# Linear attention feeding a SiLU layer: 64-position blocks with paired heads, a planned order, and casting transfers

## The chip, the cores and the metric

The kernel runs on one core of a Trainium2 chip. The metric is the device time of one execution in microseconds, the median of several runs; lower is better. The names of the engines are those of the profile: PE multiplies matrices (PEld loads its weights), DVE, ACT and POOL work on elements, SP only issues transfers. ACT and POOL can issue transfers too. Each engine takes its instructions in the order in which the program lists them.

## The reference

Two computations follow each other. The first is attention with a decay per head, worked off in blocks of positions with a state carried from block to block; the second is a two-layer network on its output. Inputs and output are float32; batch 4, 8 heads, 768 positions, 64 features per head, then 3072 rows of 512 features with 2048 in between.

```python
for b in range(nb):                                   # block = 64 positions
    intra = einsum('bhic,bhjc->bhij', qb, kb) * Dmask # lam ** (i - j) where i >= j, else 0
    intra = einsum('bhij,bhjd->bhid', intra, vb)
    inter = einsum('bhid,bhde->bhie', qb * lam_pow, kv_state)   # lam ** (i + 1)
    out[:, :, sl] = intra + inter
    kv_state = lam ** 64 * kv_state + einsum('bhsd,bhse->bhde', kb * rev_pow, vb)  # lam ** (63 - s)
x = out.transpose(0, 2, 1, 3).reshape(3072, 512)
h = x @ w_in
result = (h * sigmoid(h)) @ w_out
```

## The kernel before

**Units.** The work is cut into 24 units u of 128 positions with all 8 heads: four batches of six. The kernel takes 128 positions as one attention block, which is the same function as two blocks of 64. Two heads share the 128 partitions, so there are four pairs (NP = 4).

**Per unit.** `load` (L60) issues three transfers of 256 KB on SP (q, k, v in float32, runs of 64 features, 256 bytes each). `prep` multiplies q and k by powers of lam into bf16 on DVE (L157, L159) and copies v into a zero-padded tile on ACT (L161). `T` transposes q and k on PE, 8 times 128 columns (L169), and ACT copies the result out (L174, and L178 into the zero-padded `kTz`). `ST` computes scores per head, 8 matmuls of 128 columns (L193), and DVE applies the mask (L199). `OUT` multiplies scores by v, 8 matmuls (L217), adds the carried state, 4 matmuls except in a batch's first unit (L221), and ACT copies the sum into `xt` (L229), the activations of the network, transposed. `STATE` computes the new state in 4 matmuls (L245); DVE adds the old one (L254, L256) and POOL scales it (L260, L263); a batch's last unit has no state to pass on.

**The network.** Positions are taken in chunks of 512, four units. `gemm1` makes one 128-feature slice of the hidden layer: four matmuls of 512 columns (L278), then Silu on ACT (L284). `gemm2` makes 128 rows of output: 16 matmuls of 512 columns (L297), a copy on DVE (L303) and a store on SP (L305).

**Weights.** They are loaded as float32 on SP in eight pieces of 1 MB (L70, L75) into four staging buffers and cast to bf16 by DVE (L144, L147). A staging buffer comes free when its cast is done.

**Order.** It is written by hand: four units of attention first, then the first product for chunk 0 mixed with units 4 to 7, then for each chunk n the first product of n, the second of n - 1 and the attention of the units of n + 1, item by item. PSUM's 8 banks are dealt out for good: transposes 1, scores 2, outputs 1, state 1, first product 2, second 1.

```python
cast_w_in(0)
run(g1(0, range(0, 2)))
...
for n in range(1, NCH):
    for t in range(UPC):
        u = (n + 1) * UPC + t
        if u < NU:
            run(both(n, t), unit(u))
```

Of the kernel before, what the change touches and what calls it, by code (L numbers as in the profile page):

```python
# [7 lines left out]
F32 = mybir.dt.float32  # L8
BF16 = mybir.dt.bfloat16
AF = mybir.ActivationFunctionType  # L10
AL = mybir.AluOpType


@with_exitstack
def kernel(
# [13 lines left out]
    BLK = 128  # L29
    NB = S // BLK  # L30
    NU = B * NB
    NP = H // 2
    DM = moe_w_in.shape[0]
    DFF = moe_w_in.shape[1]
    assert DM == H * D == 512 and DFF == 2048
    KI = DM // 128
    KO = DFF // 128
    CH = 512
    NCH = B * S // CH
    UPC = CH // BLK  # L40

    ctx.enter_context(tc.manual_schedule())
    const = ctx.enter_context(tc.tile_pool(name="const", bufs=1))
    raw = ctx.enter_context(tc.tile_pool(name="raw", bufs=8))
    stage = ctx.enter_context(tc.tile_pool(name="stage", bufs=4))
    work = ctx.enter_context(tc.tile_pool(name="work", bufs=3))
    gpool = ctx.enter_context(tc.tile_pool(name="gpool", bufs=36))
    opool = ctx.enter_context(tc.tile_pool(name="opool", bufs=3))
    ps = ctx.enter_context(tc.tile_pool(name="ps", bufs=1, space=bass.MemoryType.PSUM))


    raws = {}

    def load(u):
        b, blk = divmod(u, NB)
        sl = slice(blk * BLK, (blk + 1) * BLK)
        tiles = []
        for name, src in (("qf", q), ("kf", k), ("vf", v)):
            t = raw.tile([128, H, 64], F32, tag=name, name=name)
            nc.sync.dma_start(out=t, in_=src[b, :, sl, :].rearrange("h s d -> s h d"))  # L60
            tiles.append(t)
        raws[u] = tiles

    w_in_r = moe_w_in.rearrange("(ko p) f -> p ko f", p=128)
    w_out_r = moe_w_out.rearrange("(ko p) f -> p ko f", p=128)
    wstage = {}

    def load_w_in(j):
        t = stage.tile([128, KI, 512], F32, tag="wst", name="w_st")
        nc.sync.dma_start(out=t, in_=w_in_r[:, :, j * 512:(j + 1) * 512])  # L70
        wstage["i", j] = t

    def load_w_out(j):
        t = stage.tile([128, 4, DM], F32, tag="wst", name="w_st")
        nc.sync.dma_start(out=t, in_=w_out_r[:, 4 * j:4 * j + 4, :])  # L75
        wstage["o", j] = t

    lam_sb = const.tile([128, H], F32)
    nc.sync.dma_start(
# [3 lines left out]
    for u in range(4):  # L83
        load(u)
    load_w_in(0)
    load_w_in(1)
    load(4)
    load_w_in(2)
    load(5)
    load_w_in(3)  # L90
    load(6)
    load(7)


    iota_i = const.tile([128, 1], mybir.dt.int32)
    nc.gpsimd.iota(iota_i, pattern=[[0, 1]], base=-64, channel_multiplier=1)
    pos = const.tile([128, 1], F32)
    neg = const.tile([128, 1], F32)
    nc.vector.tensor_copy(pos, iota_i)
    nc.vector.tensor_scalar(neg, pos, -1.0, None, op0=AL.mult)  # L100
    ident = const.tile([128, 128], BF16)
# [5 lines left out]
    mask = const.tile([128, BLK], F32)  # L107
    nc.gpsimd.memset(mask, 1.0)
    nc.gpsimd.affine_select(
        out=mask, in_=mask, compare_op=AL.is_ge, fill=0.0,  # L110
        base=0, pattern=[[1, BLK]], channel_multiplier=-1,
    )

    NKT, NVP, NX = 3, 4, 2
    kTz = [const.tile([128, NP, 2, BLK], BF16, name=f"kTz{i}") for i in range(NKT)]
    vz = [const.tile([128, NP, 4, 64], BF16, name=f"vz{i}") for i in range(NVP)]
    Xz = [const.tile([128, NP, 128], BF16, name=f"Xz{i}") for i in range(NX)]
    for i in range(max(NKT, NVP, NX)):
        if i < NKT:
            nc.vector.memset(kTz[i], 0.0)  # L120
        if i < NVP:
            nc.gpsimd.memset(vz[i], 0.0)
        if i < NX:
            nc.gpsimd.memset(Xz[i], 0.0)

    log_lam = const.tile([128, H], F32)
    nc.scalar.activation(log_lam, lam_sb, AF.Ln)
    lam_fwd = const.tile([128, H], F32)
    lam_bwd = const.tile([128, H], F32)
    nc.scalar.activation(lam_fwd, log_lam, AF.Exp, scale=pos[:, 0:1])  # L130
    nc.scalar.activation(lam_bwd, log_lam, AF.Exp, scale=neg[:, 0:1])
    lam_blk = const.tile([128, NP, 64], F32)
    for hh in range(2):
        r = slice(64 * hh, 64 * hh + 64)
        nc.scalar.activation(
            lam_blk[r, :, :], log_lam[r, hh::2][:, :, None].to_broadcast([64, NP, 64]),
            AF.Exp, scale=float(BLK),
        )

    w_in_bf = const.tile([128, KI, DFF], BF16)  # L140
    w_out_bf = const.tile([128, KO, DM], BF16)

    def cast_w_in(j):
        nc.vector.tensor_copy(w_in_bf[:, :, j * 512:(j + 1) * 512], wstage["i", j])  # L144

    def cast_w_out(j):
        nc.vector.tensor_copy(w_out_bf[:, 4 * j:4 * j + 4, :], wstage["o", j])  # L147


    qs, ks, qT, sts, Xf = {}, {}, {}, {}, {}  # L150
    xts = {}

    def prep(u):
        qf, kf, vf = raws.pop(u)
        qs[u] = work.tile([128, H, 64], BF16, tag="qs", name="qs")
        ks[u] = work.tile([128, H, 64], BF16, tag="ks", bufs=4, name="ks")
        nc.vector.tensor_tensor(  # L157
            qs[u], qf, lam_fwd[:, :, None].to_broadcast([128, H, 64]), op=AL.mult)
        nc.vector.tensor_tensor(  # L159
            ks[u], kf, lam_bwd[:, :, None].to_broadcast([128, H, 64]), op=AL.mult)  # L160
        nc.scalar.activation(  # L161
            vz[u % NVP][:, :, 0:4:3, :], vf.rearrange("p (a b) d -> p a b d", b=2), AF.Copy)

    def T(u):
        out_l = []
        tr = ps.tile([128, 2 * NP, BLK], BF16, tag="tr", name="tr")
        for i in range(2 * NP):
            src = (qs if i < NP else ks)[u].rearrange("p (a b) d -> p a (b d)", b=2)
            out_l.append((1, lambda i=i, src=src: nc.tensor.transpose(  # L169
                tr[:, i, :], src[:, i % NP, :], ident)))  # L170

        def evac():
            qT[u] = work.tile([128, NP, BLK], BF16, tag="qT", name="qT")
            nc.scalar.activation(qT[u], tr[:, 0:NP, :], AF.Copy)  # L174
            kz = kTz[u % NKT]
            for hh in range(2):
                r = slice(64 * hh, 64 * hh + 64)
                nc.scalar.activation(kz[r, :, hh, :], tr[r, NP:2 * NP, :], AF.Copy)  # L178
        out_l.append((0, evac))
        return out_l  # L180

    def ST(u):
        out_l = []
        kz = kTz[u % NKT]
        for half in range(2):
            box = {}

            def first(box=box):
                box["ps"] = ps.tile([128, 4, BLK], F32, tag="st", bufs=2, name="st_ps")
            out_l.append((0, first))  # L190
            for i in range(4):
                h = 4 * half + i
                out_l.append((1, lambda i=i, h=h, box=box: nc.tensor.matmul(  # L193
                    box["ps"][:, i, :], lhsT=kz[:, h // 2, h % 2, :], rhs=qT[u][:, h // 2, :],
# [246 lines left out]
```

## Time and profile before

| what | value |
|---|---|
| median of 3 runs | 256.36 us (255.65 to 257.78) |
| span of the profiled execution, first to last instruction | 254.5 us |
| HBM read, written | 27.27 MB, 6.29 MB |
| DMA packets | 82,722, of which 75,536 under 512 bytes |
| PE, 512-column matmuls (L278, L297) | 384 and 384 |
| PE, 128-column matmuls | 736 |
| ACT, Silu (L284) | 96 x 596 ns |

The profile is of one execution. Its span runs from the first to the last instruction of the program; of the execution as timed only the runs above are given. Busy times are the union of an engine's instructions; a matmul's listed length (379 ns for 512 columns) contains its way through the array, in which the next one already runs, so the listed lengths of PE add up to more than its time. A row of groups names the line, the engine, the operation, output and inputs, the count and shape, then busy time, mean length in ns, and idle time before it with what ended it.

### The profile page before, as it was taken

Reading aid. Unit: us, or ns where it says so; the run is one execution under the profiler, and the core shown is the slowest. Engines: PE = TensorE matmul, PEld = TensorE weight load, DVE = VectorE, ACT = ScalarE, POOL = GpSimd, SP = SyncE. Lnnn points to the kernel's source line nnn. Section 1 sums busy time; section 2 is a strip of 40 time slices with the busy share of each in tenths; the row PEclk is TensorE's granted clock in tenths of the full one; section 3 lists DMA queues with packets and bytes.
Section 4 is the critical chain, followed back from the end, with each engine's and each line's share of the span. In section 5 each row is a group of like instructions: output and inputs, shape, how many; then the busy total and the mean of one; then the engine's idle time right before and its main releaser. Section 6 shows DMA issues by size and latency. Waiting matters only on the chain.

```text
span 254.5 us, 3814 instructions
## 1 busy us (share of the span) xinstructions
PE 219.0 (86%) x1504; PEld 120.7 (47%) x1504; DVE 117.9 (46%) x173; ACT 126.9 (50%) x224; POOL 56.7 (22%) x71
## 2 busy tenths in 40 slices
PE   0664875937785999999999999999999999999994
PEld 0553343515442555555555555555555544444441
DVE  3586648357808537362574382537632410111221
ACT  6566374646643465656555755665465333333000
POOL 8056402004404411040343120404421200000000
PEclk9999597988999999999999999999999999999999
DMA  6999999999999994466347110111011101111122
GB/s 131 219 260 321 279 267 230 342 197 284 222 265 212 237 254 117 94 169 152 79 101 165 44 41 1 45 41 44 0 41 44 39 2 41 44 41 41 41 85 82
DMA packets 82722, 33.81 MB, mean 133 GB/s; under 512 B 75536, under 2 KB 75536, under 8 KB 82704
## 3 DMA queue, kind: packets, MB, share of 16 engines
q1 hardware_dynamic: 82704, 33.57, 55.0%
q8 instruction: 12, 0.20, 0.3%
q14 instruction: 6, 0.05, 0.1%
HBM read 27.27 MB, written 6.29 MB: 132 GB/s over the span
## 4 chain that ended last, share of the span: by engine, by line
PE 66%; DVE 1%; ACT 0%; issue 0%
PE o_ps L297 26%; PE h_ps L278 25%; PE st_ps L297 5%; PE x_ps L217 3%; PE st_ps L193 2%; PE tr L169 2%; PE x_ps L221 1%; PE d_ps L245 1%; DVE o_sb L303 1%; DVE st_sb L199 1%; ACT g L284 0%; ACT xt L229 0%
## 5 line engine op out<-in xcount | busy, mean ns | idle before, releaser
L278 PE MATMUL h_ps<-xt,w_in_bf 128*128 128x512 bf16 x384 | 119.0, 392 | 9.9 <-ACT g L284 7.2
L284 ACT ACTIVATE g<-h_ps 128x512 bf16<-128x512 f32 x96 | 57.2, 596 | 80.7 <-PE h_ps L278 80.3
L297 PE MATMUL o_ps<-w_out_bf,g 128*128 128x512 bf16 x320 | 91.4, 379 | 2.1 <-DVE w_out_bf L147 1.9
L260 POOL TENSOR_TENSOR Xz<-y,lam_blk 64x256 bf16<-64x256 f32 x40 | 34.4, 861 | 141.9 <-DVE y L256 88.3
L278 PEld LDWEIGHTS <-w_in_bf 128*128 128x128 bf16 x384 | 38.2, 100 | 44.0 <-issue 6.9
L297 PEld LDWEIGHTS <-g 128*128 128x128 bf16 x384 | 37.4, 98 | 43.9
L217 PE MATMUL x_ps<-st_sb,vz 128*128 128x128 bf16 x192 | 37.1, 227 | 8.6 <-DVE st_sb L199 7.5
L193 PE MATMUL st_ps<-qT,kTz 128*128 128x128 bf16 x192 | 36.4, 231 | 4.5 <-ACT kTz L178 4.2
L199 DVE TENSOR_TENSOR st_sb<-st_ps,mask 128x512 bf16<-128x512 f32 x48 | 31.3, 686 | 9.3 <-PE st_ps L193 8.8
L256 DVE TENSOR_TENSOR y<-d_ps,Xf 64x256 f32<-64x256 f32 x32 | 13.5, 422 | 41.0 <-PE d_ps L245 35.1
L303 DVE COPY o_sb<-o_ps 128x512 f32<-128x512 f32 x20 | 13.8, 691 | 31.8 <-PE o_ps L297 31.7
L178 ACT ACTIVATE kTz<-tr 64x512 bf16<-64x512 bf16 x48 | 28.1, 586 | 0.6
L157 DVE TENSOR_TENSOR qs<-qf,lam_fwd 128x512 bf16<-128x512 f32 x24 | 19.6, 817 | 15.1 <-DMA qf<-in_q_dram 12.2
L217 PEld LDWEIGHTS <-vz 128*128 128x128 bf16 x192 | 18.5, 102 | 14.1 <-issue 7.5
L159 DVE TENSOR_TENSOR ks<-kf,lam_bwd 128x512 bf16<-128x512 f32 x24 | 24.1, 1003 | 2.4 <-DMA kf<-in_k_dram 2.3
L193 PEld LDWEIGHTS <-kTz 128*128 128x128 bf16 x192 | 18.3, 103 | 12.6 <-ACT kTz L178 6.5
L169 PE MATMUL tr<-ident,qs 128*128 128x128 bf16 x96 | 17.8, 232 | 6.2 <-DVE qs L157 6.2
L161 ACT ACTIVATE vz<-vf 128x512 bf16<-128x512 f32 x24 | 15.1, 629 | 12.2 <-DMA vf<-in_v_dram 12.2
L174 ACT ACTIVATE qT<-tr 128x512 bf16<-128x512 bf16 x24 | 14.3, 595 | 9.5 <-PE tr L169 9.4
L169 PE MATMUL tr<-ident,ks 128*128 128x128 bf16 x96 | 17.4, 227 | 0.2 <-DVE ks L159 0.2
L221 PE MATMUL x_ps<-qT,Xz 128*128 128x128 bf16 x80 | 17.0, 219 | 0.3
L263 POOL TENSOR_TENSOR Xf<-y,lam_blk 128x256 f32<-128x256 f32 x16 | 16.6, 1036 | 1.3
(32 smaller groups left out, 108.6 us busy)
## 6 DMA issues: line engine op xcount, KB each, us to landing
qf<-in_q_dram SPq DMA_DIRECT2D x24, 256.0 KB, 5.0
kf<-in_k_dram SPq DMA_DIRECT2D x24, 256.0 KB, 5.1
vf<-in_v_dram SPq DMA_DIRECT2D x24, 256.0 KB, 5.1
out_dram<-o_sb SPq DMA_DIRECT2D x24, 256.0 KB, 2.0
w_st<-in_moe_w_in_dram SPq DMA_DIRECT2D x4, 1024.0 KB, 7.4
w_st<-in_moe_w_out_dram SPq DMA_DIRECT2D x4, 1024.0 KB, 7.9
lam_sb<-in_lam_dram SPq DMA_DIRECT2D x1, 4.0 KB, 2.8
```

What stands on the lines that cost most here:

```text
L157: nc.vector.tensor_tensor(qs[u], qf, lam_fwd[:, :, None].to_broadcast([128, H, 64]), op=AL.mult)
L159: nc.vector.tensor_tensor(ks[u], kf, lam_bwd[:, :, None].to_broadcast([128, H, 64]), op=AL.mult)
L169: out_l.append((1, lambda i=i, src=src: nc.tensor.transpose(tr[:, i, :], src[:, i % NP, :], ident)))
L178: nc.scalar.activation(kz[r, :, hh, :], tr[r, NP:2 * NP, :], AF.Copy)
L193: out_l.append((1, lambda i=i, h=h, box=box: nc.tensor.matmul(box["ps"][:, i, :], lhsT=kz[:, h // 2, h % 2, :], rhs=qT[u][:, h // 2, :], s ...
L199: nc.vector.tensor_tensor(t, box["ps"], mask[:, None, :].to_broadcast([128, 4, BLK]), op=AL.mult)
L217: out_l.append((1, lambda p=p, hh=hh, h=h: nc.tensor.matmul(box["ps"][:, p, :], lhsT=vp[:, p, hh, :], rhs=sts[u, h // 4][:, h % 4, :], sta ...
L221: out_l.append((1, lambda p=p: nc.tensor.matmul(box["ps"][:, p, :], lhsT=Xz[u % NX][:, p, :], rhs=qT[u][:, p, :], start=False, stop=True)))
L260: nc.gpsimd.tensor_tensor(xz[r, :, r], y[r], lam_blk[r], op=AL.mult)
L278: out_l.append((1, lambda ko=ko: nc.tensor.matmul(box["ps"], lhsT=w_in_bf[:, ko, m * 128:(m + 1) * 128], rhs=xts[n][:, ko, :], start=(ko = ...
L284: nc.scalar.activation(gs[n, m], box["ps"], AF.Silu)
L297: out_l.append((1, lambda ko=ko: nc.tensor.matmul(box["ps"], lhsT=gs[n, ko][:, t * 128:(t + 1) * 128], rhs=w_out_bf[:, ko, :], start=(ko = ...
```

## The change

**Attention in blocks of 64.** A unit stays 128 positions, but is computed as two blocks c of 64. For k and v, the 128 partitions now hold 64 positions of two heads, one head in each half; `kb` and `vb` are bf16 tiles whose off-diagonal halves are zero, so that one matmul serves a pair of heads: a weight of 128 x 128, block-diagonal, and a right-hand side of 64 columns. Scores are 8 such matmuls per unit, outputs 8, states 8 (4 in a batch's last unit), carried states 8 (4 in its first). The decay moves from q and k into the mask, into `lam_k` on v (`vd`, DVE) and into `lam_x` when the output is copied into `xt` (DVE).

**Transfers.** k and v of a unit come in 4 transfers of 64 KB each on SP, cast to bf16 on DVE or ACT into `kb` and `vb`. q and all eight pieces of the weights are transferred by POOL straight into bf16 tiles. For units 0 to 7 q and k are transposed on PE (12 times 128 columns); from unit 8 on two transposing transfers on SP do it, from SBUF to SBUF. Stores are issued by ACT.

**Groups.** The first product is done for groups of 1, 1, 1, 1, 2, 2, 2, 2, 4, 4, 4 units, with 128, 256 or 512 columns per matmul, four, two or one slices of the hidden layer to a PSUM bank. The second product of the last unit is split into two halves of 256 columns, each with its own copy.

**Order.** Every matmul, copy and transfer is a task with a key (its place in a rough order of units), the engines that may do it with a duration for each, what it depends on, and the buffers it holds. A list scheduler in the kernel's code walks through these with its own clock and, whenever an engine is free, takes the ready task with the lowest key; the tasks are then issued in that order. It also picks the engine where there is a choice. PSUM's 8 banks are one pool.

```diff
+    LAT = {"PE": 0.23, "ACT": 0.06, "DVE": 0.06, "POOL": 0.08, "SP": 0.0}
...
+    TURNED = 8
+    POOLS = dict(bank=8, qb=8, kf=6, vf=6, kb=4, qkT=4, vb=5, vd=4, st=3, xb=4, y=3, xf=3,
+                 xt1=4, xt2=2, xt4=2, g=40, osb=4)
...
-            nc.sync.dma_start(out=t, in_=src[b, :, sl, :].rearrange("h s d -> s h d"))
+            nc.sync.dma_start(out=t[halves[h], c], in_=src[b, h, s0 + 64 * c:s0 + 64 * c + 64])
+            nc.gpsimd.dma_start(out=fixed_tile(bufs[0]), in_=q[b, :, s0:s0 + U, :].rearrange("h s d -> s h d"))
...
-        t = stage.tile([128, KI, 512], F32, tag="wst", name="w_st")
-        nc.sync.dma_start(out=t, in_=w_in_r[:, :, j * 512:(j + 1) * 512])
-        nc.vector.tensor_copy(w_in_bf[:, :, j * 512:(j + 1) * 512], wstage["i", j])
+                nc.gpsimd.dma_start(out=w_in_bf[:, :, cs], in_=w_in_r[:, :, cs])
+                nc.gpsimd.dma_start(out=w_out_bf[:, 4 * j:4 * j + 4, :], in_=w_out_r[:, 4 * j:4 * j + 4, :])
+    sequence = ["u0", "u1", "i0", "u2", "i1", "u3", "i2", "i3", "u4", "u5", "o0", "u6", "o1", "u7", "o2", "o3"]
+    sequence += [f"u{u}" for u in range(8, NU)]
...
+    groups = [[0], [1], [2], [3], [4, 5], [6, 7], [8, 9], [10, 11]] + [list(range(4 * n, 4 * n + 4)) for n in range(3, NU // 4)]
...
+            if u < TURNED:
+                    nc.tensor.transpose(t[:, j - n0, :], turn_source(j), ident)
+            else:
+                    nc.sync.dma_start_transpose(t_of()[:, n0:n1, :], i.rearrange(
+                        "p h d -> p (h d)" if src is qb else "p i g d -> p (i g d)"))
...
-                    box["ps"][:, i, :], lhsT=kz[:, h // 2, h % 2, :], rhs=qT[u][:, h // 2, :],
+            nc.tensor.matmul(t[:, c, a, :], lhsT=t_of()[:, 4 + NP * c + a, :],
+                             rhs=t_of()[:, a, 64 * c:64 * c + 64], start=True, stop=True)
+            mult(e, tile_of(st, [128, 2, NP, 64], BF16, "st"), st_ps.tile,
+                 mask[:, None, :, :].to_broadcast([128, 2, NP, 64]))
+            nc.tensor.matmul(t[:, c, a, :], lhsT=fixed_tile(kb)[:, i],
+                             rhs=vd.tile[:, i, :], start=True, stop=True)
...
+                prev = add((s + ko / 16, 2), {"PE": w / 2400 + 0.0025}, lambda e, ko=ko, f=mm: f(e, ko),
+                           deps=[ta, prev] + wload["o", ko // 4], bufs=[bank, g])
+                nc.scalar.dma_start(out=out[128 * u:128 * u + 128, cs], in_=osb.tile[:, cs])
...
+    for _, _, e, t in plan.order():
+        t.fn(e)
```

The core of the scheduler, cut:

```python
for e in free:
    ...
    while ready[e]:
        key, i, t = heapq.heappop(ready[e])
        ...
        if any(len(self.pools[p]) < n for p, n in need.items()):
            kept.append((key, i, t))
            continue
        mine = now + t.on[e]
        if any(max(free[o], now) + d < mine - 1e-9 for o, d in t.on.items() if o != e):
            kept.append((key, i, t))
            continue
        took = t
        break
    ...
    free[e] = now + t.on[e]
    t.end = free[e] + self.LAT[e]
    if t.nbytes:
        dma = max(dma, free[e] + 1.3) + t.nbytes / t.rate
        t.end = dma + 0.7
```

## The prediction

> **What bounds the kernel now.** I read the first two parts of the page, then the costliest groups, the windows, and the timeline of PE and of the SP queue.
>
> ```profile
> span 254.5 us, 3814 instructions
> ...
> PE 219.0 (86%) x1504; PEld 120.7 (47%) x1504; DVE 117.9 (46%) x173; ACT 126.9 (50%) x224; POOL 56.7 (22%) x71
> ...
> PE   0664875937785999999999999999999999999994
> ...
> PEclk9999597988999999999999999999999999999999
> DMA  6999999999999994466347110111011101111122
> ```
>
> PE is ragged up to about 85 us, while DMA is full, and solid afterwards. The windows (columns: PE, PEld, DVE, ACT, POOL busy us with counts, granted clock, DMA share, GB/s):
>
> ```profile
> 0.00:26.00 26.00, 11.59 (x124) 9.06 (x124) 16.64 (x30) 16.49 (x28) 13.93 (x26) 0.97 1.11 232
> 26.00:58.00 32.00, 22.42 (x147) 12.54 (x148) 18.00 (x23) 17.27 (x32) 4.41 (x4) 0.82 1.03 265
> 58.00:90.00 32.00, 24.46 (x193) 14.30 (x192) 20.86 (x29) 15.90 (x30) 11.35 (x12) 0.99 1.14 242
> 90.00:215.00 125.00, 124.75 (x877) 68.75 (x876) 56.85 (x85) 69.51 (x123) 27.02 (x30) 1.00 0.30 75
> 215.00:250.00 35.00, 35.00 (x163) 15.84 (x162) 4.84 (x7) 7.76 (x13) 0.00 (x0) 1.00 0.14 53
> ```
>
> From 90 to 250 us PE waits for nothing. What a matmul occupies there is the distance to the next start, not its listed length: 0.216 us for 512 columns, 0.056 us for 128. The page counts 768 of the first (384 + 320 + 64) and 736 of the second: 165.9 + 41.2 = 207.1 us of PE work. The last matmul ends at 250.8 us, so 250.8 - 207.1 = **43.7 us are lost, all before 90 us** (the granted clock, 0.82 in the second row, is part of it), and 3.7 us follow the last matmul. Whatever gains must cut PE work or that early loss.
>
> **The change part by part.**
>
> *PE, products.* Same columns, other cuts. Two starts give a straight line in columns (128: 0.056, 512: 0.216), so 256 take 0.109. First product: 4 groups of one unit, 256 x 0.056 = 14.3; 4 pairs, 256 x 0.109 = 27.9; 3 fours, 192 x 0.216 = 41.5; together 83.7. Second: 23 x 16 x 0.216 = 79.5, and the last unit in halves 32 x 0.109 = 3.5; 83.0. Before: 165.9; after: 166.7.
>
> *PE, attention.* 192 transposes become 8 units x 12 = 96, 5.4 us. The other 544 matmuls of 128 columns become 736 of 64 (scores 192, outputs 192, states 4 x (5 x 8 + 4) = 176, carried 4 x (4 + 40) = 176), each still with a 128-column weight load. No 64-column matmul stands in the trace. The line gives 0.029; no gain from the narrower right-hand side would be 0.056. Between them one place speaks:
>
> ```profile
> 16.83 0.39 PE L245 MATMUL d_ps<-vz,ks 128*128 128x128 bf16 x4
> 17.01 0.10 PEld L193 LDWEIGHTS <-kTz 128*128 128x128 bf16 x1
> 17.05 0.22 PE L193 MATMUL st_ps<-qT,kTz 128*128 128x128 bf16 x1
> ```
>
> The four L245 started 0.056 apart, the last at 17.00. The next load began only at 17.01, yet its matmul went at 17.05, its regular turn. So a load needs at most 0.04 us before its matmul. I take 0.034, between 0.029 and 0.04: 736 x 0.034 = 25.0 us. Sum after: 166.7 + 5.4 + 25.0 = **197.1 us**, 10.0 less than before; with 0.029, 193.4; with 0.056, 213.3, which is more than before.
>
> The Trainium skill, "TensorE: Matmul & The Clock Gate", section "LDWEIGHTS (loading the stationary operand)", gives a load of P columns P/1.2 ns, 107 ns here. Matmuls that each bring a load start 56 ns apart in this trace, so the measurement speaks against that figure. By it the 736 would take 78.5 us and the run 276 us.
>
> *Start.* What feeds it is DMA:
>
> ```profile
> 7.00 1.14 SPq L60 DMA_DIRECT2D qf<-in_q_dram  x1
> 8.19 1.10 SPq L60 DMA_DIRECT2D kf<-in_k_dram  x1
> 9.32 1.32 SPq L60 DMA_DIRECT2D vf<-in_v_dram  x1
> 10.69 1.14 SPq L60 DMA_DIRECT2D qf<-in_q_dram  x1
> ```
>
> A unit (three loads of 256 KB) goes through in 3.6 us. For weights: up to 76 us the GB/s of the windows add up to 19.2 MB; less 8.4 MB of weights that is 13.7 units, 49.5 us, leaving some 24.5 us for 8 weights, 3.07 each. The new order u0 u1 i0 u2 i1 u3 i2 i3 u4 u5 o0 u6 o1 u7 o2 o3 then lands, from 2 us on: i0 at 12.3, u3 at 22.5, u4 at 32.3, o3 at 55.3. What PE can do per unit, by the prices above: attention 1.05 + 0.67 of transposes = 1.7; a quarter of the first product 0.9; of the second 0.86. Before u3 is there, that is three units' attention (5.1) and two quarters for three units (5.4): 10.5 us. Lost at that point: landing 22.5, plus the way from landing to `xt`, less 10.5. The way: the sum of bare rows (cast 0.42, transposes 0.4, copy out 0.7, scores 0.3, mask 0.69, outputs 0.3, `xt` 0.69, handing on) is 4 us; before, unit 0's v landed at 7.5 and its `xt` began at 15.4, 8 us. I take 7: 19 us. The other points give less (u4: 32.3 + 7 - 21.2 = 18). With some queueing I put the **loss at 20 us** in place of 43.7; its ends are 12 (landing alone) and 43.7 (nothing won). Most of the gain is that the first product starts per unit, not per four units after L144's cast, and that no weight waits for a staging buffer (the last is issued only at 67.94 us now) or for DVE: PE's waits there (L144 2.5, L147 1.9) and 10.4 us of DVE casts go.
>
> What must stay hidden: early DVE and ACT work. Per unit: casts of k and v 4 x 0.42 (a quarter of L144's 1.39 plus a start), scaled v 0.69 to 1.0, copies out of the transposes about 1.1, mask 0.69, states 0.84, spreading 4 x 0.29, `xt` 0.69, 7 us together, and Silu 4 x 0.6: 9.4 us on two engines, 4.7 each, against 6.7 us per unit (53.3 / 8) that DMA needs with the weights. It fits, but not loosely: each us that these engines need per unit beyond 6.7 would add 8 us over the 8 early units.
>
> *Queues.* SP gets 192 loads of 64 KB and 32 transposing transfers instead of 105 transfers. The shortest SP issue is 0.33 to 0.43 us, so 8 loads cost 2.9 us per unit, less than 3.6. A transposing transfer waits for its cast, and the next units' loads stand behind it; those have 8.2 us of PE work per unit (197.1 / 24) to hide in. No transposing row exists; the same bytes as a load take 1.14 + 0.57 = 1.7 us per unit, below zero is excluded since PE's share of it is already counted. I take that, hidden. ACT gets the stores: 25 x 0.4 = 10 us of an engine busy half the time; Silu stands behind each. POOL gets 32 issues; nearest rows: SP's 0.4, POOL's own longest operation 1.59 and a load's landing 5.0. I take 1.6: 16 of them, 26 us, end long before 55.3. One table load (1.28 us) goes.
>
> *End.* The last copy is halved: 0.69 to 0.42, so 3.4 us after the last matmul.
>
> *Sum.* 197.1 + 20 + 3.4 = 220.5 us of span, and 0.7 for small waits of the new order (the old one has none after 90 us): 221.2. Only the span of the profiled execution is given; the median of the timed runs, 256.36, lies 1.8 above 254.5. So **223 us**.
>
> **The rivals.**
>
> *Weight loads set the pace.* If a 64-column matmul takes 0.056 us, PE work is 213.3 and the time 239. For it: every load is still 128 columns and listed with 98 ns. Against it: the 0.04 above. 0.10. The page's 107 ns, which the trace contradicts, has 0.01 and 276.
>
> *POOL holds up the start.* If a casting transfer occupies POOL until it lands, at 5.0 us for q and 7.4 to 7.9 for weights (the page's landing times), q6 lands at 2 + 7 x 5.0 + 4 x 7.4 + 7.9 = 74.5 us, when 37 us of work have been enabled, and the loss becomes 74.5 + 7 - 37 = 44.5: 247 us. For it, POOL's Xf takes 0.73 us at 20.02 with DVE elsewhere and 1.59 at 27.12 behind a DVE cast:
>
> ```profile
> 25.07 3.06 DVE L144 CAST w_in_bf<-w_st 128x2048 bf16<-128x2048 f32 x2
> ...
> 27.12 1.59 POOL L263 TENSOR_TENSOR Xf<-y,lam_blk 128x256 f32<-128x256 f32 x1
> ```
>
> Against it: those weight casts go, and the remaining ones are 0.4 us. The Trainium skill, "SBUF — State Buffer", section "SBUF: two separate sides", says that GpSimd cannot write descriptors while VectorE runs a two-port copy; the trace agrees so far that POOL's work doubles. 0.13.
>
> *Transposing transfers bind: slower.* If each holds the SP queue until it has landed (5.1 us, the landing of 256 KB), a unit costs SP 2 x 5.1 + 2.9 = 13.1 us against 8.2 of PE. 16 units from 55 us on, then 36 (the last four units' products 28, the way to `xt` and the end 8): 55 + 210 + 36 = 301 us. It decides from (256 - 91) / 16 = 10.3 us per unit, 3.7 per transfer. For it: SP blocked 5.26 us on one load at 18.08. Against it: there it was queued behind weights on a full DMA; later DMA is at 0.30. 0.08.
>
> *The order is no better.* The written-in durations miss and PE, which takes its instructions in order, waits at heads of lists as much as before: 197.1 + 43.7 + 3.4 + 1.8 = 246 and 10 us of new waits spread over 24 units, 256. Nothing after 90 us hints at it. 0.05.
>
> **How the numbers follow.** Forecast 0.60 at 223; weight pace 0.10; POOL 0.13; transposing 0.08; no better 0.05; 107 ns 0.01; a start better than 211, 0.03. Low end: 0.029 (-3.7) and a loss of 12 (-8): 211. High end: 247, with the POOL rival in. About a sixth is left out (transposing, no better, 107 ns, a better start). Measurement of this kernel tells about 1% from no change: faster 0.60 + 0.10 + 0.13 + 0.03 = 0.86; same 0.04 (most of "no better"); slower 0.10.
>
> **What would show it.** Starts of 64-column matmuls 0.03 to 0.04 apart; first product beginning near 13 us; PE solid from about 50 us; POOL issues under 3 us; SP never the last releaser of a score matmul after 60 us; DMA full to about 55 us. The forecast is wrong if PE has holes after 60 us, or if scores wait for `qkT`.

## The result, and the profile after

The changed kernel takes **283.31 us** (median of 4 runs, 282.12 to 284.6), the kernel before 256.0 us on the same chip (4 runs): a ratio of 1.104, interval 1.097 to 1.111. The forecast was 223 us, with 0.86 for faster; the time lies above the range and on the other side.

First the page of the changed kernel: span, busy times, the 40 slices, the queues, and the two lines of the chain that ended last.

```profile
span 282.9 us, 5054 instructions
...
PE 214.6 (76%) x1936; PEld 133.9 (47%) x1936; DVE 116.7 (41%) x251; ACT 123.8 (44%) x233; POOL 44.1 (16%) x65
...
PE   0563997998089961986620199999999999999994
...
PEclk9998797999659995699595589999999999999999
DMA  7999999994465499458456597997451001010113
...
q1 hardware_dynamic: 77824, 18.89, 38.6%
q0 software_dynamic: 29184, 7.34, 26.3%
...
PE 37%; SPq 7%; DMA 3%; DVE 2%; issue 2%; ACT 1%; ACTq 0%; DVEq 0%
```

Before, PE was ragged to 85 us and solid afterwards. Now it has holes up to the 23rd slice (163 us), whole slices at 0 to 2 tenths among them, and is solid only from there. The windows (the columns as before) show where:

```profile
26.00:58.00 32.00, 26.43 (x390) 22.43 (x391) 20.12 (x42) 16.80 (x32) 8.92 (x11) 0.85 1.54 175
58.00:90.00 32.00, 22.25 (x218) 15.78 (x216) 15.05 (x33) 12.80 (x24) 2.15 (x3) 0.84 0.59 125
90.00:120.00 30.00, 21.46 (x157) 12.59 (x156) 11.43 (x27) 10.58 (x20) 5.05 (x6) 0.83 0.91 132
120.00:150.00 30.00, 17.42 (x193) 12.12 (x191) 12.98 (x29) 10.73 (x21) 1.22 (x2) 0.86 0.60 123
150.00:180.00 30.00, 17.78 (x163) 12.30 (x163) 10.33 (x22) 11.50 (x21) 4.34 (x5) 0.74 0.73 126
180.00:215.00 35.00, 34.81 (x360) 19.26 (x358) 27.95 (x57) 26.07 (x52) 8.20 (x11) 1.00 0.78 131
```

None of the five columns is near full between 58 and 180 us, and where PE is short, DVE, ACT and POOL are short too. That is the look of everybody waiting for one late thing, not of a busy engine.

The prediction's two quantities can be read again. PE's work is **193.4 us**: 64-column matmuls start 29 ns apart (median of 602 neighbouring pairs of one line), and 128, 256 and 512 columns keep 56, 109 and 216 ns. The last matmul starts at 278.65 us, so 85.2 us are lost, where before it was 43.6 (43.7 in the forecast, counted to the end of the last matmul). The loss up to a time is that time less the work of the matmuls started by then:

| us | 30 | 60 | 70 | 80 | 90 | 120 | 140 | 160 | 180 | end |
|---|---|---|---|---|---|---|---|---|---|---|
| before | 21.1 | 34.9 | 38.8 | 42.3 | 43.3 | 43.4 | 43.3 | 43.4 | 43.2 | 43.6 |
| after | 23.9 | 31.8 | 32.4 | 41.6 | 43.4 | 54.7 | 62.7 | 80.6 | 84.8 | 85.2 |

Three pieces, then: about 32 us up to 60 us, 9 us in one hole at 70 to 80, and 42 us after 90, of which before had none. In the terms of the forecast's sum: PE work 193.4 us for 197.1, loss 85.2 for 20 and 0.7 of small waits, and 4.2 from the last start to the end, together 282.9 us of span.

**The late piece.** The longest hole ends at 161.7 us. The chain of waits leading to it (start, length, what):

```profile
142.56 0.61 SPq L277
143.28 1.27 SPq L371
144.65 1.23 SPq L371
145.98 0.60 SPq L277
...
157.06 3.28 DMA qkT<-kb
160.51 0.56 issue
161.07 0.61 ACT osb L244
161.72 2.04 PE h_ps L497 x9
```

SP issues almost without a pause, 0.61 us for a 64 KB load and 1.25 for a transposing transfer, until the transposing transfer at 157.06; when that has landed, ACT casts its `kb`, copies an output, and PE goes on. What ACT and DVE did meanwhile is in their waits (in total, times, longest):

```profile
ACT kb L244 <- DMA qkT<-kb: 37.5, 4, 21.3
...
ACT g L510 <- DMA kf<-in_k_dram: 9.5, 1, 9.5
```

```profile
DVE kb L246 <- DMA qkT<-kb: 37.3, 4, 20.5
```

```profile
PE h_ps L497 <- ACT osb L244: 18.7, 1, 18.7
```

The cast of a later unit's k into `kb` stands at the head of both queues. There are four `kb` tiles; the one that it wants is still the source of a transposing transfer, and that transfer stands in SP's queue behind the loads of yet later units. Behind the cast, in the same in-order queues, stand the copy and the Silus that would free a PSUM bank for PE. So SP's lateness reaches PE, though PE's next work needs nothing from SP. PE's two other long waits after 90 us follow the same casts: 8.5 us, ended at 112.3, after DVE had stood 8.9 us at a `kb`, and 4.0 us, ended at 136.7, after ACT had stood 5.0.

Between 60 and 180 us SP's queue is idle for 5 us in all. The timeline of its queue gives the price:

```profile
135.25 2.57 SPq L277 DMA_DIRECT2D kf<-in_k_dram  x4
137.92 2.57 SPq L277 DMA_DIRECT2D vf<-in_v_dram  x4
140.60 2.57 SPq L277 DMA_DIRECT2D kf<-in_k_dram  x4
143.28 1.27 SPq L371 DMA_TRANSPOSE qkT<-kb  x1
144.65 1.23 SPq L371 DMA_TRANSPOSE qkT<-qb  x1
```

From one group of four to the next 2.67 us pass, 0.67 a load; with the stretches that run on, 0.64 to 0.67. A unit from 8 on costs SP 8 x 0.64 + 2 x 1.25 = 7.6 us. The scheduler in the kernel has 8 x 0.3 + 2 x 0.4 = 3.2 us for it.

**The hole at 70 us.** ACT's timeline (start, length, instruction; in brackets the idle time before and its releaser):

```profile
67.33 0.60 ACT L244 ACTIVATE osb<-o_ps 128x512 f32<-128x512 f32 x1 [0.29 <-PE o_ps L528]
67.95 0.63 ACT L244 ACTIVATE kb<-kf 64x512 bf16<-64x512 f32 x1
77.69 0.35 ACTq L545 DMA_DIRECT2D out_dram<-osb  x1
78.09 0.60 ACT L510 ACTIVATE g<-h_ps 128x512 bf16<-128x512 f32 x1 [9.51 <-DMA kf<-in_k_dram]
```

The output was copied at 67.9, and its store was issued at 77.69, when a k load had landed. In the program's list of instructions every store on ACT waits, besides for its copy, for one of eight completion counters that SP's and ACT's transfers use in turn: for a load of SP that was listed a few transfers earlier. The trace shows it here: the store and the k load issued at 75.13 carry the same counter, number 102, and that load landed at 77.62. ACT stands there, with the next Silu behind it, and PE stops for 9.1 us.

### The profile page after: what moved, and what is told of

Read it like the earlier page. It is cut to its first block, busy times and chain, and to the rows that moved or that the text cites. A ratio compares the mean times of both kernels' runs of the same rounds, so it can differ in the third digit from the quotient of the medians.

```text
span 282.9 us, 5054 instructions
## 1 busy us (share of the span) xinstructions
PE 214.6 (76%) x1936; PEld 133.9 (47%) x1936; DVE 116.7 (41%) x251; ACT 123.8 (44%) x233; POOL 44.1 (16%) x65
## 3 DMA queue, kind: packets, MB, share of 16 engines
q1 hardware_dynamic: 77824, 18.89, 38.6%
## 4 chain that ended last, share of the span: by engine, by line
PE 37%; SPq 7%; DMA 3%; DVE 2%; issue 2%; ACT 1%; ACTq 0%; DVEq 0%
PE o_ps L528 18%; PE h_ps L497 16%; SPq L277 5%; DMA qkT<-kb 3%; SPq L371 2%; PE x_ps L451 2%; PE st_ps L381 1%; PE d_ps L400 1%; DVE y L419 1%; ACT osb L244 0%; DVE xt L251 0%; DVE vb L246 0%; DVE vd L251 0%; DVE xf L251 0%; ACTq L545 0%
## 5 line engine op out<-in xcount | busy, mean ns | idle before, releaser
L497 PE MATMUL h_ps<-xt,w_in_bf 128*128 128x128 bf16 (+2 forms) x704 | 123.1, 297 | 20.2 <-ACT osb L244 18.7
L528 PE MATMUL o_ps<-w_out_bf,g 128*128 128x512 bf16 (+1 forms) x400 | 116.6, 384 | 0.0
L497 PEld LDWEIGHTS <-w_in_bf 128*128 128x128 bf16 x704 | 62.7, 104 | 49.1 <-issue 21.4
L510 ACT ACTIVATE g<-h_ps 128x512 bf16<-128x512 f32 x96 | 54.7, 595 | 53.5 <-PE h_ps L497 43.5
L244 ACT ACTIVATE xb<-y 64x256 bf16<-64x256 f32 x54 | 22.2, 414 | 20.2 <-DVE y L419 10.3
L280 POOL DMA_DIRECT2D qb<-in_q_dram x24 | 22.0, 917 | 25.4 <-PE tr L358 8.7
L251 DVE TENSOR_TENSOR st<-st_ps,mask 128x512 bf16<-128x512 f32 x24 | 16.5, 688 | 20.5 <-PE st_ps L381 20.3
L244 ACT ACTIVATE osb<-o_ps 128x512 f32<-128x512 f32 (+1 forms) x22 | 12.6, 574 | 21.1 <-PE o_ps L528 20.6
L419 DVE TENSOR_TENSOR y<-d_ps,xf 128x256 f32<-128x256 f32 x40 | 16.7, 419 | 10.6 <-ACT xb L244 4.2
L251 DVE TENSOR_TENSOR xt<-x_ps,lam_x 128x512 bf16<-128x512 f32 x24 | 16.4, 685 | 4.6 <-PE x_ps L451 4.3
L251 DVE TENSOR_TENSOR vd<-vf,lam_k 128x512 bf16<-128x512 f32 x24 | 16.8, 705 | 1.5 <-DMA vf<-in_v_dram 1.2
L400 PEld LDWEIGHTS <-kb 128*128 128x128 bf16 x176 | 10.4, 103 | 13.6 <-ACT kb L244 6.8
L358 PEld LDWEIGHTS <-kb 128*128 128x128 bf16 x64 | 5.1, 118 | 20.0 <-issue 15.9
## 6 DMA issues: line engine op xcount, KB each, us to landing
out_dram<-osb ACTq DMA_DIRECT2D x23, 256.0 KB, 2.3
```

Of the source, the lines that this page charges most:

```text
L244: nc.scalar.activation(o, i, AF.Copy)
L251: (nc.vector if e == "DVE" else nc.gpsimd).tensor_tensor(o, a, b, op=AL.mult)
L280: nc.gpsimd.dma_start(out=fixed_tile(bufs[0]), in_=q[b, :, s0:s0 + U, :].rearrange("h s d -> s h d"))
L358: nc.tensor.transpose(t[:, j - n0, :], turn_source(j), ident)
L400: nc.tensor.matmul(t[:, c, a, :], lhsT=fixed_tile(kb)[:, i], rhs=vd.tile[:, i, :], start=True, stop=True)
L419: nc.vector.tensor_tensor(t, d_ps.tile[:, c], xf[0].tile, op=AL.add)
```

## The experiments

Eighteen variants of the changed kernel. "Loss" is the start of the last matmul less the PE work, which is 193.4 us, or 204.1 where all units are transposed on PE. In some traces 1 to 2% of the matmul records are missing; losses up to an earlier time are then up to 2 us high and marked with a tilde. Most times are of one run and say no more than about 1%; the first twelve were taken beside runs of the kernel before of 259.1 us (t24, price, kb8, vact), 254.9 (spool, gate, and both that join t24, price and stores on POOL) and 256.7 (the other four). Since these differ, the ratio is to the runs of the kernel before beside which each was taken. "Plan" is where the scheduler's own clock ends when it is run on the host.

| edit | time, us | ratio | plan, us | loss | up to 60 | up to 90 |
|---|---|---|---|---|---|---|
| (the changed kernel) | 283.3 | 1.104 | 220.0 | 85.2 | 31.8 | 43.4 |
| t24: all transposes on PE | 261.9 | 1.011 | 229.4 | 51.8 | ~33 | ~44 |
| price: SP's real prices in the plan | 262.3 | 1.012 | 227.5 | 62.8 | ~35 | ~49 |
| kb8: eight `kb` tiles | 272.5 | 1.052 | 219.5 | 73.1 | ~32 | ~47 |
| vact: v loads on ACT | 290.4 | 1.121 | 219.8 | 91.0 | ~56 | ~67 |
| spool: stores on POOL | 281.8 | 1.106 | 220.0 | 81.4 | ~32 | ~35 |
| gate: weights held back | 294.9 | 1.157 | 224.5 | 95.6 | ~41 | ~45 |
| plainw: weights through SP | 311.2 | 1.212 | 266.8 | 111.8 | ~41 | ~56 |
| price + plainw | 265.4 | 1.034 | 231.9 | 66.1 | ~38 | ~48 |
| t24 + price + stores on POOL | 276.7 | 1.086 | 249.7 | 65.3 | ~32 | ~42 |
| the same + gate | 288.0 | 1.130 | 260.8 | 75.6 | ~45 | ~58 |
| t24 + price | 277.6 | 1.081 | 246.7 | 67.5 | ~36 | ~54 |
| t24 + price + stores on SP | 278.9 | 1.086 | 247.3 | 68.9 | ~32 | ~43 |
| t24 + stores on POOL | 262.1 | 1.012 | 229.4 | 53.1 | 31.4 | 34.1 |
| the same, attention a unit later | 262.3 | 1.014 | 227.5 | 50.7 | 31.1 | 33.2 |
| t24, a quarter of the weights' bytes | 245.1 | 0.947 | 229.4 | 34.9 | 27.3 | 28.6 |
| t24, v loads on POOL | 267.6 | 1.034 | 233.6 | 57.0 | 32.7 | 49.2 |
| price + stores on POOL | 264.6 | 1.031 | 227.5 | 63.1 | 32.4 | 38.6 |
| the same, Xf on DVE | 263.2 | 1.027 | 227.5 | 62.3 | 31.1 | 38.0 |

### SP's queue: transposes off it, its real prices, more tiles, loads elsewhere

```diff
-    TURNED = 8
+    TURNED = 24
```

> All 24 units transposed on PE, so SP carries only the 192 loads of k and v (0.64 us each in the trace of the changed kernel, 5.2 us per unit). PE work rises by 16 x 12 x 0.056 = 10.7 us to 204.1. Theory (SP falls behind the planned order; the casts of later units, in ACT's and DVE's queues ahead of Silu, wait for kb tiles that transposing transfers still hold): the loss of 42 us after 90 us is gone, time 245 to 258. Rival (the loss comes from the casting transfers or from DMA's own speed): still 280 or more, up to 294.

261.9 us, above the theory's 245 to 258, but the loss after 90 us falls from 42 to about 8 us. With the transposing transfers the late piece is gone; the scheduler made another order, too, so which of the two did it is not separated here.

```diff
-            return [add((key, i), {"SP": 0.3}, ...
+            return [add((key, i), {"SP": 0.65}, ...
-                turned.append(add((u - 200.0, 9), {"SP": 0.4}, dma_turn, ...
+                turned.append(add((u - 200.0, 9), {"SP": 1.27}, dma_turn, ...
```

> Only two written-in durations change: a load on SP 0.3 to 0.65 us, a transposing transfer 0.4 to 1.27, as the trace shows them. The work is the same, the order is made anew. Theory (the harm is in the order, made with SP at 40% of its real cost): PE's loss after 90 us falls from 42 to under 20, time 240 to 262. Rival (SP's capacity itself, 7.7 us per unit, or DMA, is the bound whatever the order): 275 to 290.

262.3 us with the same instructions in another order, and some 14 us are lost after 90 us: 21 us come from two numbers in the plan. But a new hole of 14.9 us is there, again at a store on ACT:

```profile
55.11 1.09 ACT L510 ACTIVATE g<-h_ps 128x512 bf16<-128x512 f32 x2
69.01 2.01 ACTq L545 DMA_DIRECT2D out_dram<-osb  x2
71.06 0.41 ACT L244 ACTIVATE xb<-y 64x256 bf16<-64x256 f32 x1 [14.87 <-DMA out_dram<-osb]
```

```diff
-    POOLS = dict(..., kb=4, qkT=4, ...
+    POOLS = dict(..., kb=8, qkT=4, ...
```

> Eight kb tiles in place of four, nothing else. Rival that too few tiles is the cause: casts no longer wait for transposing transfers (75 us of such waits on ACT and DVE now), time 240 to 260. Theory (SP is late whatever the tiles are): the wait moves to qkT and the loads, SP stays full to beyond 180 us, time 268 to 290.

The rival was that the four tiles, not SP, are the fault. The casts' waits for them fall from 75 us (both engines) to 22, but the time only to 272.5: POOL's q loads now wait 29.3 us for the other transposing transfer, that of `qb`. More tiles move the wait; the late transfer stays.

```diff
+            (nc.scalar if e == "ACT" else nc.sync).dma_start(out=t[halves[h], c], in_=...
-            return [add((key, i), {"SP": 0.3}, ...
+            return [add((key, i), {"SP" if i == 0 else "ACT": 0.3}, ...
```

> The 96 loads of v are issued by ACT, so SP has 4 x 0.64 + 2.5 = 5.1 us per unit in place of 7.7. Theory: SP keeps up, the loss after 90 us falls below 15, time 240 to 262, unless ACT's own queue delays the loads. Rival (transposing transfers themselves are slow or the start alone counts): 275 or more.

290.4 us, worse. ACT's queue began with 24 v loads, all that fit into six tiles, and came to its first copy at 48.85 us:

```profile
12.72 36.08 ACTq L277 DMA_DIRECT2D vf<-in_v_dram  x24
48.85 1.02 ACT L244 ACTIVATE qkT<-tr 128x1024 bf16<-128x1024 bf16 x1 [43.49 <-DMA vf<-in_v_dram]
```

This doesn't speak on SP's pace: an engine that computes cannot carry loads that run ahead.

### The stores

```diff
-                nc.scalar.dma_start(out=out[128 * u:128 * u + 128, cs], in_=osb.tile[:, cs])
+                nc.gpsimd.dma_start(out=out[128 * u:128 * u + 128, cs], in_=osb.tile[:, cs])
```

> Only the queue of the stores changes: POOL issues them in place of ACT, at the same places in the order. In the instruction list a store on ACT waits for one of eight counters that transfers of SP and ACT share, so for an SP load listed up to eight transfers earlier. Theory (this wait carries SP's lateness into ACT, which then holds PE): the 9 us hole of PE at 70 to 80 us goes and the holes after 100 us shrink, time 255 to 272. Rival (holes come from casts waiting for kb tiles alone): 279 to 287.

The hole at 70 to 80 us is gone, the loss at 90 us falls by 9 us as the reading of the hole asks. Yet against the kernel before beside it nothing is gained (1.106, was 1.104), as the rival had it: what PE no longer loses there, it loses later, at the casts.

### The start: are the weights too early?

```diff
+            nc.gpsimd.tensor_copy(first, vf.tile[64:65, 1, NP - 1, 63:64])
             if what == "i":
```

(one element of a given unit's v, copied on POOL into the weight tile, ahead of each weight transfer: it holds the transfer back until v is there)

> Before each weight transfer POOL copies one element of a unit's v into the place that the transfer then overwrites (units 0, 1, 2, 2 for w_in, 4, 5, 6, 6 for w_out), so weights can't run ahead of their place in the order. Theory of the early loss (POOL's weights, issued up to 20 us ahead of their turn, take half of DMA from k and v): the loss of PE work at 60 us falls from 32 to under 25; the late holes stay, time 272 to 282. Rival (SP's issue pace sets the arrival of units, or DMA is full anyway): loss at 60 us 30 to 40, time 282 to 295.

294.9 us, and 41 lost up to 60 us instead of 32. q's transfers, which nothing held back, ran ahead in the weights' place: 12 units of q had landed by 30 us, 6 in the changed kernel. Not a clean test, and no support for the theory.

```diff
-                nc.gpsimd.dma_start(out=w_in_bf[:, :, cs], in_=w_in_r[:, :, cs])
+            nc.sync.dma_start(out=tile_of(wst, [128, 4, 512], F32, "wst"), in_=frm)
+            copy(e, to[:, i:i + 2, :], wst.tile[:, i:i + 2, :])
```

> The eight weight pieces come as float32 on SP, in their place among the loads of k and v, into two staging buffers and are cast by DVE or ACT in halves; q stays a casting transfer. Theory of the early loss (POOL's queue takes two thirds of DMA's time from 10 to 50 us: 9.2 us of packets per 10 us against 4.8 for k and v): k and v of a unit pass in under 7 us where they take 8.7 now, and the loss at 60 us falls from 32 to under 27; the late holes stay (SP has more to issue), time 268 to 285. Rival (the early loss is SP's issue pace or DVE and ACT): loss at 60 us 30 or more.

> The same with SP priced at 0.65 and 1.27 us in the plan. Theory: both gains add up, loss at 60 us under 28 and under 15 later, time 236 to 252. Rival: 258 or more.

311.2 and 265.4 us. Weights as float32 through SP, cast by DVE or ACT, are in place of k and v then, and the casts stand in the two queues: `w_out`'s alone wait 37 us for their pieces in the first of the two. k and v do come sooner there (8.4 units by 60 us, not 7.2), as the theory had it, yet both lose about 40 us up to 60 us. Sending the weights another way did not shorten the start.

### Combinations

> All transposes on PE, a load on SP priced at 0.65 us in the plan, stores on POOL. PE work 204.1. Theory: no hole after 60 us is left, loss 33 to 40 in all, time 240 to 250. Rival (with 192 small loads SP stays late in any order): 258 or more.

> The same with the weights held to their place. Theory of the early loss: 6 to 10 us less than without, 232 to 242. Rival (DMA or SP bound in the start): as without, or up to 8 us more.

> All transposes on PE, a load on SP priced at 0.65 us, stores on ACT as in the changed kernel. If the store's wait for a load's counter is harmless once the plan has SP's real pace: 245 to 256. If the early loss is all that is left and stays at 45: 253 to 260. If pricing loads later in the plan harms the start: above 262.

> The same with the stores on SP, priced at 0.65 us: ACT no longer waits for a transfer's counter, SP has 5.9 us per unit of the 8.5 that PE needs. Theory: no hole of the kind at 70 to 80 us, 4 to 10 us less than with stores on ACT. Rival (a store at the head of SP's queue holds up loads): as much or more than with stores on ACT.

276.7, 288.0, 277.6 and 278.9 us: all slower than either of t24 and price alone. With stores on ACT a hole of the known kind is there (ACT stands 15.2 us at a store behind a k load); with stores on SP or POOL it is gone, and the time is no better. Nor is it the standing at stores: SP waits 107 us at its stores, all of it after its last load is issued. What the four share is a longer plan: the scheduler's own clock ends at 246.7 to 260.8 us, in t24 at 229.4 and in price at 227.5. The runs are 27 to 32 us above their plans, t24 is 32 above its own and price 35. So their extra time is planned; why the scheduler finds a longer order with these prices wasn't tried out. And the loads still come later than planned (with t24 + price 13.9 units by 100 us, where the plan has 18.5). True issue prices in the plan, then, are not enough by themselves; the theory that they are was wrong.

### What is the start made of, and do the two gains add?

The next four were taken beside runs of the kernel before of 258.7 us.

> All 24 units transposed on PE (no transposing transfers) and the stores issued by POOL instead of ACT, the order being that of the first of these alone. If transposing transfers in SP's queue and stores waiting on ACT are two separate causes, the gains add: the loss of 51.9 us with the first alone falls by about 9 (the hole at 70 to 80 us) to 43, and the time is 253 (250 to 256). If they are one cause, or POOL's own work (Xf) now waits behind stores, it stays at 262 or gets worse.

262.1 us (ratio 1.012, interval 1.006 to 1.019, to the kernel before). The hole at 70 to 80 us goes here too, 34.1 instead of 44 at 90 us, and again its time is lost later, between 90 and 160. The gains do not add.

```diff
-        s = u - 4.0 if u < 4 else u - 5.5
+        s = u - 4.0 if u < 4 else u - 4.5
```

> The same, with attention placed one unit nearer to its product in the order (u - 4.5 instead of u - 5.5 from unit 4 on). If casts and copies of far-ahead units, standing in DVE's and ACT's queues before their loads have come, cost PE ready work, the loss by 90 us falls by 5 us or more against t24_spool, and the time with it. If loads alone set the start, it stays within 2 us; then, too, holes may come back later because attention is now late.

33.2 us at 90 instead of 34.1, 50.7 in all instead of 53.1: within 2 us by 90. Where attention stands in the rough order matters little.

```diff
-                nc.gpsimd.dma_start(out=w_in_bf[:, :, cs], in_=w_in_r[:, :, cs])
+                nc.gpsimd.dma_start(out=w_in_bf[:, 0:1, cs], in_=w_in_r[:, 0:1, cs])
+                nc.gpsimd.memset(w_in_bf[:, 1:4, cs], 0.0)
```

> All 24 units transposed on PE, and of each weight piece only a quarter is transferred; POOL fills the other three quarters with zeros (so the products are computed with zeros there). Order and number of issues are as with the transposes on PE alone. If a full DMA sets the start, 6.3 MB less free some 20 us of it, k and v come sooner, and the loss at 60 us falls from 32.7 to under 22. If SP's pace of issues (5.2 us for a unit's eight loads) or the order sets it, the loss at 60 us stays at 28 to 33.

245.1 us, with three quarters of the weights left out. The loss at 60 us is 27.3, below the band of SP and order and above that of a full DMA. The zeros kept POOL busy for 25 of the first 26 us, with q's transfers behind them, so the first 40 us (26.2 lost, t24 24.9) are no clean test. After 60 us PE hardly stops (7.6 us more to the end, t24 19):

```profile
PE   0052799999999999999994999999999999999993
...
PEclk9999999999999999999999999999999999999998
DMA  5999996977499589935454511011011011111122
```

> All 24 units transposed on PE, and v's 96 loads issued by POOL instead of SP, so that SP issues only k (2.6 us per unit) and POOL 4 x 0.8 + 0.9 = 4.1 us per unit beside the weights. If SP's pace of issues sets the start, the loss at 60 us falls from 32.7 to about 25. If the DMA engines' time sets it, it stays within 3 us; if POOL becomes the late one, v comes after k and the loss rises.

267.6 us, 32.7 up to 60: SP's pace by itself is not the start. Later POOL is the late one: a DVE addition waits 18.5 us for an Xf that stands on POOL behind loads.

This pair of results asks for a count: how much has landed, and how much of PE's work does it allow? A unit's k and v are 2048 packets of 256 bytes, its q 1024 packets of 128, a weight piece 512 of 1024, so the packets that have ended give the units (a transposing transfer's packets have 256 bytes too and are taken off by SP's order of issue); the work of these units (attention, and both products of every group that is whole, with the weights landed) against the work done gives:

| us | units of k and v landed, after | work allowed, us | done, us | landed, t24 | landed, fewer weights | landed in the plan's own clock |
|---|---|---|---|---|---|---|
| 30 | 3.1 | 16.3 | 6.1 | 3.1 | 4.7 | 3 |
| 60 | 7.2 | 53.2 | 28.2 | 7.1 | 10.0 | 8 |
| 80 | 10.6 | 84.5 | 38.4 | 10.6 | 13.5 | 13 |
| 100 | 13.6 | 101.2 | 56.7 | 14.3 | 17.0 | 18 |
| 120 | 16.0 | 131.6 | 65.3 | 17.6 | 20.4 | 21 to 24 |

The last column is what the scheduler, run on the host, writes down for the ends of v's loads (24 at 120 us in t24's plan). After 40 us transfers are not what PE lacks: at 60 us data for 53 us of work is there and 28 us are done. But loads come later than the plan has them (8 units at 60, 18 at 100), and an engine whose list was made for the planned times stops at whatever is not there yet. With fewer bytes loads are ahead of the plan at 60 and 80 us and not far behind at 100, and the holes are gone; order and issues are t24's. Three edits bear on that. Price changes the order alone, and fewer weights, against t24, the bytes; in both the loads come nearer to their plan at 100 us (1.7 units late, 4.5 in the changed kernel; 1.5, 4.2 in t24), and the loss after 60 us falls. T24 leaves the loads as late as they were and takes the transposing transfers out of SP's queue, so the dearest part is what waited for those. Lateness against the lists is the cause as far as these runs show it; the share of each piece is not separated.

Where SP falls behind, its own waits say (the changed kernel):

```profile
SPq L277 <- DMA kf<-in_k_dram: 9.3, 12, 1.4
SPq L277 <- DMA vf<-in_v_dram: 7.4, 13, 1.2
```

All but 0.2 us of these lie before 60 us. A load takes the counter of the eighth transfer before it and waits until that one has landed, and the DMA engines are full then. In t24 the two waits are 13.9 us up to 60, with fewer weights 1.3, and by 60 us 7.5 and 10.4 units are issued; from 60 to 100 us both issue 7.0 units. So SP loses its lead at full DMA engines, and its price per issue keeps it from winning it back.

### Can the rest be had?

> SP's real prices in the plan (0.65 and 1.27 us) and the stores issued by POOL, in the order of the plan with the prices alone. If the store at which ACT stands is a loss of its own, the hole of 14.9 us at 56 to 71 us goes and the loss falls from 62.8 us to about 49: 193.4 + 49 + 4 + 1.8 = 248 us, below the 256 of the kernel before. If Xf now waits behind stores on POOL, holes come back between 80 and 160 us and the time stays at 258 to 266.

> The same with Xf on DVE alone, so that POOL has nothing but memsets and transfers and no engine that PE waits for stands behind a store. If Xf behind stores is what takes the gain back, this one is faster than price_spool by 3 us or more: 245 us (240 to 252). If DVE's 42 more operations of 0.42 us make DVE late, or if nothing waited for Xf, it is the same or slower than price_spool.

264.6 and 263.2 us (ratios 1.031, 1.025 to 1.037, and 1.027, 1.020 to 1.034). The hole of 14.9 us is gone, and its time is lost between 80 and 160 us:

```profile
PE   0425779988996609699697989989999999999992
```

Xf behind stores is 1 us, not the reason. Here too the loads are behind the plan: it has 14 units by 100 us and 17 by 120, the run 12.7 and 14.1, and by 100 us PE had done 54.2 us of work and the plan 70.6. The plan knows the price of an issue now, but not the 17 us up to 60 that SP waits for its own loads to land: by 60 us it has issued 10.9 units, the run 7.5. Scores wait for `qkT` six times, 13.8 us in all. A plan with that wait in it, and with PE's slower clock after holes (below), wasn't tried out. No variant that computes everything is faster than the kernel before.

## Why the prediction was wrong, step by step

- **PE work: right, at its low end.** 193.4 us; 0.029 us per 64-column matmul where 0.034 was taken. "Weight loads set the pace" is refuted. The forecast read the Trainium skill's P/1.2 ns for a weight load ("TensorE: Matmul & The Clock Gate", section "LDWEIGHTS (loading the stationary operand)") as a pace, and as a pace it fails: 107 ns, where the loads of 128 columns go 29 ns apart here. As the length of one load it is close: the page of the changed kernel lists them with 101 to 104 ns in four of its five groups. This step says the change is worth 13.7 us.
- **Queues, SP: the step that failed.** "The shortest SP issue is 0.33 to 0.43 us, so 8 loads cost 2.9 us per unit" took the first issues after a pause of the queue. The rows right behind those were in the trace of before too, at 0.53 to 0.78 us for 256 KB, the few longer ones aside:

```profile
108.04 0.43 SPq L60 DMA_DIRECT2D qf<-in_q_dram  x1
108.52 0.73 SPq L60 DMA_DIRECT2D kf<-in_k_dram  x1
...
117.80 0.74 SPq L60 DMA_DIRECT2D vf<-in_v_dram  x1
```

  An issue costs 0.64 us for 64 KB and about as much for 256: cutting 48 loads of k and v into 192 multiplied the cost by nearly four, 8 x 0.64 = 5.1 us per unit instead of 2.9. "A transposing transfer ... 1.7 us per unit ... I take that, hidden" was 2.5. The sum of 4.6 is 7.6 us, still below PE's 8.2; so SP's throughput alone would have stayed hidden. What it lost is its lead: 16.5 us of waits for its own loads up to 60 us, and then an issue price that leaves no room to catch up.
- **"Hidden" was the deeper error.** I named what stands behind a transposing transfer on SP (loads), and not what stands behind the casts on ACT and DVE that wait for it: copies and Silus of other units. A lateness of SP passes through three in-order queues. The rival "transposing transfers bind" had the right place and the wrong price and bound: it wanted 10.3 us per unit for slower; 7.6 were enough, because it compared pace with pace and not lateness with the lists.
- **Stores on ACT.** "25 x 0.4 = 10 us", "Silu stands behind each": the issue is 0.35 us, but it waited 9.5 us for a load of SP. The wait was not in the sum.
- **Start: 32 us where 20 were forecast.** I let transfers land in the order in which the plan lists them, u3 at 22.5 us and o3 at 55.3. The packets say that k and v of u3 were whole only at 38.2 us, while all of `w_in` was there at 26.8 and o3 at 48.8: POOL's and SP's queues do not follow each other, they run side by side on the full DMA engines, and POOL's took about two thirds of the time. My own formula with these times gives 38.2 + 7 - 15.9 (three units' attention, 5.1, and, with all of `w_in` there, their whole first product, 10.8) = 29 us, close to the 32: what was wrong is the landing order. That the formula comes out here is one point, with its 7 us unmeasured, and no proof of it. Turning the order round doesn't help by itself: held-back weights brought u3 at 32.3 us, but the whole of `w_in` at 41.8, and 41 us were lost.
- **POOL.** Casting transfers take 0.74 to 1.11 us to issue, not 1.6. That rival's price was wrong in the harmless direction.
- **"The order is no better", 0.05.** The written-in durations did miss, and PE did wait at heads of lists; I gave it "10 us of new waits", and 42 came. The plan's own clock ends at 220.0 us, near my 223: plan and forecast rest on the same prices for SP, so agreement between them would have been no evidence.
- **What would show it.** Of the signs named for a wrong forecast the holes after 60 us are there; scores waited for `qkT` only 0.3 us, since the lateness came in by way of the casts. The first product began at 16.6 us, not near 13.

## What to carry to other kernels

Count issues, not bytes, on a queue that many loads share, and take the price of one from a stretch where they stand back to back. A static list is only as good as its latest item: price it from a trace, then compare landing times with the plan's before looking at any engine. Do not put an instruction that waits for a transfer (a cast, or a store with a shared counter) on an engine whose next instruction frees something for the bound engine, unless the transfer is early with room to spare.

## What the runs showed of the hardware

- **A hole costs more than its length.** After the 9.1 us hole PE ran at half speed until about 83.2 us, 4.5 us long: a 512-column matmul stands 0.43 us from the next start (79.55 to 79.97), twice its 0.216.

```profile
78.74 1.01 PE L358 MATMUL tr<-ident,kb 128*128 128x128 bf16 x8 [9.14 <-ACT g L510]
79.55 0.63 PE L528 MATMUL o_ps<-w_out_bf,g 128*128 128x512 bf16 x1
79.97 0.84 PE L497 MATMUL h_ps<-xt,w_in_bf 128*128 128x256 bf16 x3
...
83.89 0.38 PE L528 MATMUL o_ps<-w_out_bf,g 128*128 128x512 bf16 x1
```

  The granted clock in the trace is at half from 73.3 to 83.5 us. In all such stretches together, starts that stood less than 2.6 times their usual distance apart are 12.6 us over it, of the 85.2 lost; before it was 5.3, with fewer weights nothing. The Trainium skill, "TensorE: Matmul & The Clock Gate", section "What's actually happening", says that the array's clock halves after an idle window and comes back after about 3.4 us of work; the trace agrees, with 4.5 us here.
- **An issue has a fixed price on SP:** 0.64 us for 64 KB (before, 0.53 to 0.78 for 256 KB), 1.25 us for a transposing transfer of 128 x 512 as of 128 x 1024. The Trainium skill, "DMA: Bandwidth & Descriptors", section "Issuing engines are not separate DMA queues", calls the time to initiate a transfer usually small beside the transfer; here 192 loads and 32 transposing transfers are 163 us of one queue.
- **Casting q's short rows is slow per byte:** a packet of q (256 bytes read, 128 written) takes 32 ns after 60 us, when a plain one of 256 bytes takes 18; up to 60 us, with the engines full, both take 31. A weight packet takes 96 ns, a plain one of 2048 bytes 84 (medians). From 10 to 50 us POOL's queue has 9.2 us of packet time in every 10, and k and v have 4.7: the two together are more than 10, so packets overlap on an engine.
